# Linear attention and two MLPs on one core: the first block's attention in halves of 64 positions, and the low part of x by a matrix product

## The chip, the core and the metric

The kernel runs on one core of one Trainium2 chip. The metric is the device time of one execution in microseconds (us): 966.9 us before the change, the median of three runs (966.79 to 966.91 us).

Five engines work side by side, each through its own queue of instructions in order: PE (TensorE, matrix products into the accumulator memory PSUM), DVE (VectorE) and ACT (ScalarE) for element-wise work, POOL (GpSimd, here only constants), and SP (SyncE), which issues the transfers. Semaphores order them.

## What is computed

```python
def attn(q, k, v, alpha):                 # B=4, H=8, S=768, D=48
    state = zeros((B, H, D, D))
    for t in range(S):
        state = alpha[:, :, t, :, None] * state + einsum('bhd,bhe->bhde', k[:, :, t], v[:, :, t])
        y[:, :, t] = einsum('bhd,bhde->bhe', q[:, :, t], state)
x = y as (3072, 384)
x = ((x @ w_a) * (x @ w_b)) @ w_out       # 384 -> 1536 -> 384
h = x @ w_in                              # 384 -> 2048
out = (max(h, 0) + beta * min(h, 0)) @ w_out2
```

## The kernel before

**Blocks and chunks.** The 3072 tokens are worked in 6 blocks of 512. A block holds 4 chunks of 128 positions, one for each of the 4 sequences of the batch, so that the chunks of a block do not depend on each other and each takes its state from the chunk of the same sequence in the block ahead. The attention of a chunk comes first (`chunk`, L359), then the two products of the first MLP over the whole block (`pa`, `pb`), then its third (`acc`); after all blocks, the second MLP runs over weights that were written to memory in between.

**Two parts of a number.** The large products are made in a fast format (fp32r), so each operand is a high part, which is the rounded number, and a low part, which is what is left; one product of 128x512 is three matrix products (high times high, low times high, high times low: L699, L700, L702). The weights arrive as 64-bit numbers and are cut into these parts by `conv` (L231): an ACT operation, four DVE operations, an ACT rounding, and then the low part, which is made on DVE, or, for the first unit of each weight (the list `ON_PE`), by three products with the identity on PE (L308 to L310) and an ACT copy. Two of these first units are worked in halves of 384 columns (`halves`).

**A chunk.** DVE makes two scans of the decay (L402, L412) and multiplies k and q by them (L417). PE transposes k (`kps`, L453), ACT copies it out (`ks`). PE multiplies k with q (`A`), DVE masks the result (`As`), PE multiplies it with v (`y`), adds the state's part (`inter`), and computes the chunk's state sum (`dS`). ACT rounds y to the high part of x (`split_h`, L657), DVE subtracts it for the low part (`split_l`, L661).

**Three kinds of block.** Blocks 1 to 5 work a chunk in two halves of 64 positions: `pe_cross` (each half's own key rows against the other head group, and the two half states), then `z1`, the state in the chunk's middle (`mid`, DVE), then `pe_own` (L558 again, then L565 with Z, then L565 with z1). The array's four quarters are used at once: a product on 64 partitions in and 64 out takes one quarter, and in these loops two following indices change the quarter each time. Block 0 has no state to start from and takes each chunk whole: `A` over 128 columns (L471), `pe_d` (L528) and `pe_y` (L544, and L548 with `vg`, a copy of v that holds the fourth group's rows where the first three leave room). Block 0 thus needs no fourth group of 128 rows; block 1 moves the fourth group into these places by a product with `shift` (L611), and the later blocks by transfers (L677).

**What sets the order.** Nothing is scheduled by hand. Each operation is handed to a planner (`Graph`) with an engine, an estimated duration and a key; it walks its estimates and emits each engine's queue in that order. Where PE would be idle for over 500 ns by its estimates, it emits small products on a constant (`wp`, L185), up to the start of block 2, for about 0.7 of the gap that it expects. They are emitted as ordinary work: on the chip they run whether PE would have waited or not.

**Where the first block's buffers are.** In block 0 `kps`, and the two halves of `A`, use the three banks that later accumulate the MLP (`acc0` to `acc2`); `y` uses a pair of banks of its own, one pair for all chunks, held until the low part of x is made.

Of the kernel before, what the change touches and what calls it, by code (L numbers as in the profile page):

```python
# [11 lines left out]
F32 = mybir.dt.float32  # L12
# [9 lines left out]
P = 128  # L22
# [117 lines left out]
def body(tc, akq, v, vg, w_a, w_b, w_o1, w_in, w_o2, beta, out):  # L140
# [13 lines left out]
    with ExitStack() as ctx:  # L154
# [12 lines left out]
        mask = const.tile([P, P], F32, name="mask")  # L167
# [10 lines left out]
        def fill(t0, t1):  # L178
# [13 lines left out]
        nc.gpsimd.affine_select(  # L192
            out=mask, in_=mask, pattern=[[1, P]], compare_op=ALU.is_ge, fill=0.0,
            base=0, channel_multiplier=-1,
        )
# [28 lines left out]
        def conv(src, tag, name, key, wait, sink, early=15000, on_pe=False, halves=None):  # L224
# [14 lines left out]
            for n in range(2 if halves else 1):  # L239
# [29 lines left out]
                def rest(c2=c2, word=word):  # L269
                    o = c2()  # L270
                    nc.vector.scalar_tensor_tensor(out=o, in0=word(0, U32), scalar=2.0**-52,
                                                   in1=c2(), op0=ALU.mult, op1=ALU.mult)

                def high(n=n, c1=c1, hi=hi):
                    if n == 0:
                        b["r"] = wpool.tile([P, 2 * UC], F32R, name=f"w{name}", tag=tag)
# [24 lines left out]
                for h in range(2 // N):  # L301
# [3 lines left out]
                    def add(p=p, cut=cut, c1=c1, c2=c2, hi=hi):  # L305
# [4 lines left out]
                        nc.tensor.matmul(o, ident, cut(c2()), start=False, stop=True)  # L310
# [5 lines left out]
                    y = G.add("PE", 1600, add, key, [x], pool=mpool)  # L316
# [37 lines left out]
        def chunk(g):  # L354
            s = st[g]
            n, c = divmod(g, BC)
            start, moved, end = n == 0, n == 1, n == NB - 1
# [40 lines left out]
            lv = A("SP", 1250 if start else 720, load_v, vring.take(), 12000, 3000)  # L398
# [66 lines left out]
            def pe_a():  # L465
                if start:
                    s["A"] = [b(f"A{i}") for i, b in enumerate(abanks)]
                    for j in range(NJ):
                        for i in range(2):
                            ps = slice(64 * i, 64 * i + D)  # L470
                            nc.tensor.matmul(s["A"][i][:, j, :], kT()[ps, j, :], qT()[ps, j, :],  # L471
                                             start=True, stop=True)
                    return
# [10 lines left out]
            def ev_a(i):  # L484
                def f():
                    if i == 0:
                        s["At"] = tp.tile([P, 2 * NJ * CH], F32, name="As", tag="As", bufs=1)
                        w = CH if start else HC
                        s["As"] = s["At"][:, 0 : 2 * NJ * w].rearrange("p (i j t) -> p i j t", i=2, j=NJ)
                    if start:  # L490
                        m = mask.rearrange("p (o t) -> p o t", o=1).to_broadcast([P, NJ, CH])
                        nc.vector.tensor_tensor(out=s["As"][:, i], in0=s["A"][i], in1=m, op=ALU.mult)
                        return
                    m = mask[:, 0:HC].rearrange("p (a o t) -> p a o t", a=1, o=1).to_broadcast([P, 2, NJ, HC])
                    a = s["A"].rearrange("p i (j t) -> p i j t", t=HC)
                    nc.vector.tensor_tensor(out=s["As"], in0=a, in1=m, op=ALU.mult)
                return f

            w = sring.take()
            if start:  # L500
                (b0, w0, h0), (b1, w1, h1) = bank(1), bank(2)
                abanks = (b0, b1)
                pa = A("PE", 1200, pe_a, [k1, q1, *w0, *w1])
                a0 = A("DVE", 660, ev_a(0), [pa, *w])
# [517 lines left out]
```

## Time and profile before

| what | before |
|---|---|
| median of 3 runs | 966.9 us (966.79 to 966.91) |
| the profiled execution, its own time | 966.85 us |
| its span, first to last instruction | 965.2 us |
| PE busy | 952.7 us, 99% of the span |
| DVE busy | 600.4 us, 62% |
| ACT busy | 253.9 us, 26% |
| granted TensorE clock, mean | 0.999 |

The time outside the span is 1.65 us. A row of the timeline gives the start, the duration, the engine, the line of the code, the operation, and what it writes and reads; xN is the number of instructions merged into it. A PE duration includes the pipeline behind the last instruction, so the cost of a group of PE work is taken from its start to the next group's start. An fp32 product leaves two records, so 8 of them show as x16.

### The profile page before, as it was taken

To read this page: it belongs to the slowest core of one execution; us is meant where nothing else is said; L and a number is where in the kernel's file an instruction comes from. 1 tells how busy PE (TensorE), PEld (TensorE's weight loads), DVE (VectorE), ACT (ScalarE), POOL (GpSimd) and SP (SyncE) were. 2 spreads that over 40 slices of the span, in tenths; PEclk is the share of its full clock that TensorE was granted. 3 is DMA by queue.
4 is the path that set the end of the run, shared out by engine and by line. 5 is a ranking of instruction groups with operands and counts; after the bars stand their busy time and mean duration, and the time that the engine had idled before them with its cause. 6 is when DMAs were issued, how large, how long until landed. Compare 5 with 4: busy or idle time off the path is not lost.

```text
span 965.2 us, 15549 instructions
## 1 busy us (share of the span) xinstructions
PE 952.7 (99%) x6667; PEld 770.4 (80%) x6667; DVE 600.4 (62%) x887; ACT 253.9 (26%) x422; POOL 4.4 (0%) x18
## 2 busy tenths in 40 slices
PE   6999999999999999999999999999999999999998
PEld 5778888778877887887788888888888888888886
DVE  7999888578668868865332254555555545545554
ACT  2444443233333333332221211111111111111111
POOL 1000000000000000000000000000000000000000
PEclk9999999999999999999999999999999999999999
DMA  8971000145456545742065550010100200200000
GB/s 317 407 287 51 12 1 12 45 145 180 150 179 204 206 167 191 240 153 79 25 210 197 196 196 1 27 72 1 65 33 1 89 10 0 99 1 1 33 1 33
DMA packets 31076, 104.09 MB, mean 108 GB/s; under 512 B 3488, under 2 KB 4256, under 8 KB 31008
## 3 DMA queue, kind: packets, MB, share of 16 engines
q1 hardware_dynamic: 30864, 102.97, 30.2%
q8 instruction: 52, 0.85, 0.4%
q10 hardware_dynamic: 144, 0.13, 0.0%
q14 instruction: 16, 0.13, 0.0%
HBM read 74.78 MB, written 26.74 MB: 105 GB/s over the span
## 4 chain that ended last, share of the span: by engine, by line
PE 99%; DVE 0%; DMA 0%; ACT 0%; issue 0%; DVEq 0%; ACTq 0%
PE acc L699 12%; PE acc L702 12%; PE acc L700 12%; PE pi L699 7%; PE pi L702 7%; PE pi L700 7%; PE pb L699 5%; PE pa L699 5%; PE pa L700 5%; PE pb L700 5%; PE pb L702 5%; PE pa L702 5%; PE wp L185 2%; PE y L558 2%; PE kps L453 1%; PE A L481 1%
## 5 line engine op out<-in xcount | busy, mean ns | idle before, releaser
L722 ACT CAST gh<-ng 128x512 fp32r<-128x512 f32 x96 | 59.6, 621 | 328.6 <-DVE ng L935 275.0
L931 DVE TENSOR_SCALAR ng<-pi,betaT 128x512 f32<-128x512 f32 x96 | 72.1, 751 | 106.7 <-PE pi L702 105.8
L726 DVE TENSOR_TENSOR gl<-ng,gh 128x512 fp32r<-128x512 f32 x96 | 66.3, 691 | 79.9 <-ACT gh L722 79.9
L699 PE MATMUL pi<-x,v 128*128 128x512 f32 x288 | 113.3, 393 | 0.0
L700 PE MATMUL acc<-gh,v 128*128 128x512 f32 x288 | 113.1, 393 | 0.0
L702 PE MATMUL acc<-gl,v 128*128 128x512 f32 x288 | 112.9, 392 | 0.0
L700 PE MATMUL pi<-x,v 128*128 128x512 f32 x288 | 112.7, 391 | 0.0
L699 PE MATMUL acc<-gh,v 128*128 128x512 f32 x288 | 112.1, 389 | 0.0
L829 DVE TENSOR_TENSOR a_sb<-a_sb,pb 128x512 f32<-128x512 f32 x72 | 49.4, 686 | 96.5 <-PE pb L702 96.4
L699 PE MATMUL pa<-x,wa 128*128 128x512 f32 x216 | 86.7, 401 | 0.0
L699 PE MATMUL pb<-x,wb 128*128 128x512 f32 x216 | 86.6, 401 | 0.0
L699 PE MATMUL acc<-gh,wo 128*128 128x512 f32 x216 | 86.6, 401 | 0.0
L702 PE MATMUL acc<-gl,wo 128*128 128x512 f32 x216 | 84.9, 393 | 0.0
L700 PE MATMUL pa<-x,wa 128*128 128x512 f32 x216 | 84.7, 392 | 0.0
L700 PE MATMUL pb<-x,wb 128*128 128x512 f32 x216 | 84.6, 392 | 0.0
L700 PE MATMUL acc<-gh,wo 128*128 128x512 f32 x216 | 84.6, 392 | 0.0
L826 ACT COPY a_sb<-pa 128x512 f32<-128x512 f32 x72 | 42.2, 587 | 151.0 <-PE pa L702 151.0
L702 PE MATMUL pi<-x,v 128*128 128x512 f32 x288 | 81.5, 391 | 0.0
L722 ACT CAST gh<-a_sb 128x512 fp32r<-128x512 f32 x72 | 44.8, 622 | 102.6 <-DVE a_sb L829 102.6
L935 DVE SCALAR_TENSOR_TENSOR ng<-pi,ng 128x512 f32<-128x512 f32 x96 | 66.4, 691 | 3.1
L699 PEld LDWEIGHTS pi<-x,v 128*128 128x128 f32 x288 | 54.1, 188 | 13.7 <-DVE ng L935 2.1
L699 PEld LDWEIGHTS acc<-gh,v 128*128 128x128 f32 x288 | 54.0, 188 | 12.3
(120 smaller groups left out, 1426.5 us busy)
## 6 DMA issues: line engine op xcount, KB each, us to landing
kq<-in_akq SPq DMA_DIRECT2D x24, 512.0 KB, 3.8
w2d<-ws SPq DMA_DIRECT2D x16, 768.0 KB, 3.5
v<-w2d SPq DMA_DIRECT2D x16, 768.0 KB, 5.4
x2d<-x SPq DMA_DIRECT2D x18, 512.0 KB, 3.3
x<-x2d SPq DMA_DIRECT2D x6, 1536.0 KB, 6.9
ra<-in_akq SPq DMA_DIRECT2D x24, 258.5 KB, 3.5
v<-in_v SPq DMA_DIRECT2D x24, 256.0 KB, 4.4
rs<-in_w_in SPq DMA_DIRECT2D x8, 768.0 KB, 5.5
```

The lines of the kernel that those rows point to most:

```text
L185: nc.tensor.matmul(wp, warm[:, 0:P], warm, start=True, stop=True)
L453: nc.tensor.transpose(s["kps"][:, j, :], kT()[:, j, :], ident)
L558: nc.tensor.matmul(y_of(k, half(p), part_of(h)), s["v"][part_of(h), 2 * j + i, :], s["As"][part_of(h), i, j, :], start=first, stop=False, ...
L699: nc.tensor.matmul(o, lh, rh, start=first and n == 0, stop=False)
L700: nc.tensor.matmul(o, ll, rh, start=False, stop=False)
L702: nc.tensor.matmul(o, lh, rl, start=False, stop=last and n == len(pairs) - 1)
L722: nc.scalar.copy(gq[idx][0], src())
L726: nc.vector.tensor_tensor(out=gl, in0=src(), in1=gh.bitcast(F32), op=ALU.subtract)
L826: nc.scalar.copy(b["a"], ba["t"])
L829: nc.vector.tensor_tensor(out=b["a"], in0=b["a"], in1=bb["t"], op=ALU.mult)
L931: nc.vector.tensor_scalar(out=b["n"], in0=bh["t"], scalar1=0.0, scalar2=betaT[:, i : i + 1], op0=ALU.min, op1=ALU.mult)
L935: nc.vector.scalar_tensor_tensor(out=b["n"], in0=bh["t"], scalar=0.0, in1=b["n"], op0=ALU.max, op1=ALU.add)
```

## The change

Five things are done, all of them ahead of block 2, but for one order of products that all blocks share.

1. The first units of `w_a` and `w_b` (the ones in halves) round their smallest part at once into the place of the low part, and the third product of the three on PE then takes that rounded part in the fast format, where it took an fp32 operand.
2. Block 0 works its chunks in halves of 64 like the others. `A` is made as in blocks 1 to 5, one mask operation stands where two were, the mask constant is made in halves, and the ACT copy that halved it is gone. There is no state at the start, so `inter` runs for the second half alone. The half states are separate products (`state_of`), the first in `pe_cross`, the second in `pe_own`, summed in one PSUM region; ACT copies them out (`mid`, `kept`).
3. `y` of block 0 uses the banks `acc1` and `acc2`, held until the low part of x has been copied out; the shared pair of banks holds `A`.
4. `vg` is gone, its 4 transfers and its products with it; block 0 moves the fourth group by the product with `shift`, as block 1 does.
5. In blocks 0 and 1 the low part of x is made by PE, which adds minus the high part onto y in PSUM (`less`), and ACT, which copies the result out (`ev_l`).

In `pe_own` of all blocks the order is new: the second half's `inter` for the even heads (`i` = 0, upper half of the array), the eight `intra`, the second half's `inter` for the odd heads (lower half), and then the first half's `inter`.

```diff
-                def rest(c2=c2, word=word):
-                    o = c2()
+                def rest(n=n, c2=c2, lo=lo, word=word):
+                    if n == 0 and halves:
+                        b["r"] = wpool.tile([P, 2 * UC], F32R, name=f"w{name}", tag=tag)
+                    o = lo() if halves else c2()
...
-                        nc.tensor.matmul(o, ident, cut(c2()), start=False, stop=True)
+                        rest = (plus, cut(lo())) if halves else (ident, cut(c2()))
+                        nc.tensor.matmul(o, *rest, start=False, stop=True)
...
-            start, moved, end = n == 0, n == 1, n == NB - 1
+            start, moved, end = n == 0, n <= 1, n == NB - 1
...
-                if start:
-                    s["vg"] = wpool.tile([P, KT, 2, 64], F32, name="vg", tag=f"s{c % 2}")
-                    nc.sync.dma_start(s["vg"], vg[c])
...
+            def inter(j, i, h, last):
+                k, p = slot_of_head(j, i)
+                ps = slice(64 * i, 64 * i + D)
+                z = s["z1"] if h else Z[:, c]
+                nc.tensor.matmul(y_of(k, slice(64 * p, 64 * p + D), part_of(h)), z[ps, j, :],
+                                 qT()[ps, j, part_of(h)], start=False, stop=last,
+                                 skip_group_check=True)
+
+            def state_of(h):
+                for j in range(NJ):
+                    for i in range(2):
+                        nc.tensor.matmul(s["dS"][h][half(i), j, :], s["ks"][part_of(h), j, half(i)],
+                                         s["v"][part_of(h), 2 * j + i, 0:D], start=False,
+                                         stop=j == NJ - 1, skip_group_check=True)
...
+                for j in range(NJ):
+                    for h in range(2):
+                        intra(j, 1 - h, h, j < 2)
+                if start or end:
+                    state_of(0)
+                    return
...
+            def pe_own():
+                for j in range(NJ):
+                    inter(j, 0, 1, False)
+                for j in range(NJ):
+                    for i in range(2):
+                        intra(j, i, i, False)
+                for j in range(NJ):
+                    inter(j, 1, 1, j > 1)
+                if start:
+                    state_of(1)
+                    return
+                for j in range(NJ):
+                    for i in range(2):
+                        inter(j, i, 0, j > 1)
...
-                def pe_own():
-                    for j in range(NJ):
-                        for i in range(2):
-                            intra(j, i, i, False)
-                    for h, z in ((0, Z[:, c]), (1, s["z1"])):
-                        for j in range(NJ):
-                            for i in range(2):
-                                inter(j, i, h, z, h == 1 and j > 1)
...
+            def less():
+                for x, y in two(0):
+                    nc.tensor.matmul(y, minus, x, start=False, stop=True, skip_group_check=True)
+
+            def ev_l():
+                for x, y in two(1):
+                    nc.scalar.copy(x, y)
...
-            xl = A("DVE", 700, split_l, [s["xh"]])
-            yhold.append(xl)
+            if moved:
+                xl = A("PE", 450, less, [s["xh"]])
+                xl = A("ACT", 700, ev_l, [xl])
+            else:
+                xl = A("DVE", 700, split_l, [s["xh"]])
```

How the queues change is shown at three places. PE's queue around the second chunk of block 0, before (`A_240` and `A_241` are the two banks of `A`):

```order
L453 MATMUL kps<-plus,kq 128x128 x4
L544 MATMUL y<-As,v 64x128 x6
L548 MATMUL y<-As,vg 64x128 x6
L471 MATMUL A_240<-kq 128x128
L471 MATMUL A_241<-kq 128x128
...
L528 MATMUL dS<-v,ks 64x48 x8
```

and after the change, the first chunk's `pe_cross` to its `less` (`y_211` and `y_212` are the two banks of its y; the `kps` and `A` in it belong to the second chunk):

```order
L517 MATMUL y_212<-v,ks 64x48 x8
L455 MATMUL kps<-plus,kq 128x128 x4
L475 MATMUL A<-kq 64x64 x16
L510 MATMUL y_211<-kq,As 48x64 x4
...
L510 MATMUL y_212<-kq,As 48x64 x4
L517 MATMUL y_212<-v,ks 64x48 x8
...
L584 MATMUL y_211<-shift 128x128 x2
L584 MATMUL y_212<-shift 128x128
...
L636 MATMUL y_211<-x,minus 128x256
L636 MATMUL y_212<-x,minus 128x128
```

The 12 products over `v` and `vg` became 16 `intra`, 8 `inter` and 3 `shift`; the one state became two, of 8 products each; `less` is new.

PE's queue at a chunk of a later block, its `pe_own`, before:

```order
L558 MATMUL y<-As,v 64x64 x8
L565 MATMUL y<-kq,Z 48x64 x8
L565 MATMUL y<-kq,As 48x64 x8
L453 MATMUL kps<-plus,kq 128x128 x4
L699 MATMUL pa<-x,wa_1652 128x512
```

and after:

```order
L510 MATMUL y<-kq,As 48x64 x4
L502 MATMUL y<-As,v 64x64 x8
L510 MATMUL y<-kq,As 48x64 x4
L510 MATMUL y<-kq,Z 48x64 x8
L455 MATMUL kps<-plus,kq 128x128 x4
```

The same 24 products stand in another order: the 8 over `z1` (it lies in the tile `As`) are parted in two fours, one ahead of the `intra` and one behind.

ACT's queue from the first chunk's `ks` on, before:

```order
L457 COPY ks<-kps 128x512
L630 COPY Z<-dS 128x192
L457 COPY ks<-kps 128x512
L657 CAST x<-y 128x2x128
L657 CAST x<-y 128x128
```

and after (`As<-y_212` is z1, `shift<-y_212` the fourth group that is to be moved):

```order
L459 COPY ks<-kps 128x512
L547 COPY As<-y_212 128x192
L580 COPY shift<-y_212 128x128
L603 COPY Z<-y_212 128x192
L459 COPY ks<-kps 128x512
L628 CAST x<-y_211 128x2x128
L628 CAST x<-y_212 128x128
L256 ACTIVATE c_316<-ra_192 128x3x128
L640 CAST x<-y_211 128x2x128
L640 CAST x<-y_212 128x128
```

ACT has four operations more for each chunk of block 0, and a weight conversion's first operation (L256) now stands between the rounding of x and the copy of its low part.

In the whole program PE's queue has 128 `wp` where it had 125; from the first `pa` of block 1 on, the large products stand in the same order as before, and the chunks of blocks 2 to 5 differ by `pe_own` alone.

## Rows read from the trace of the kernel before

**Rows 1.** The page's first part: busy time and share of the span.

```profile
PE 952.7 (99%) x6667; PEld 770.4 (80%) x6667; DVE 600.4 (62%) x887; ACT 253.9 (26%) x422; POOL 4.4 (0%) x18
```

**Rows 2.** Waits, whole span: who waited, for whom, us in total, times, longest.

```profile
PE kps L453 <- DVE kq L417: 8.0, 1, 8.0
```

**Rows 3.** Timeline of PE, the first 21 us: start, duration, instructions.

```profile
7.96 1.09 PE L453 MATMUL kps<-plus,kq 128*128 128x128 f32 x4 [7.96 <-DVE kq L417]
...
12.01 2.83 PE L185 MATMUL wp<-ones 128*128 128x256 bf16 x13
14.68 0.60 PE L453 MATMUL kps<-plus,kq 128*128 128x128 f32 x4
15.21 0.88 PE L544 MATMUL y<-As,v 128*64 128x128 f32 x12
...
16.67 1.16 PE L471 MATMUL A<-kq 48*128 48x128 f32 x16
17.76 0.67 PE L528 MATMUL dS<-v,ks 128*64 128x48 f32 x16
18.36 2.36 PE L185 MATMUL wp<-ones 128*128 128x256 bf16 x20
20.56 0.60 PE L453 MATMUL kps<-plus,kq 128*128 128x128 f32 x4
```

**Rows 4.** The tile wp: all its products, duration in ns, first and last start.

```profile
L185 PE MATMUL wp<-ones x125: 271/272/421, 12.0 to 89.2; 128*128 128x256 bf16 x125
```

**Rows 5.** Timeline of PE: one conversion's three products in halves.

```profile
29.18 0.91 PE L308 MATMUL cl<-c,plus 128*128 128x384 f32 x2
...
30.11 0.81 PE L310 MATMUL cl<-c,plus 128*128 128x384 f32 x2
30.75 0.49 PE L185 MATMUL wp<-ones 128*128 128x256 bf16 x3
```

**Rows 6.** Timeline of PE: A in halves, and the first large product.

```profile
34.73 0.69 PE L481 MATMUL A<-kq 48*64 48x64 f32 x32
35.35 0.51 PE L699 MATMUL pa<-x,wa 128*128 128x512 f32 x1
```

**Rows 7.** Timeline of PE: a chunk of block 1, half states and pe_own.

```profile
41.45 0.63 PE L581 MATMUL y<-v,ks 64*64 64x48 f32 x32
...
43.67 0.46 PE L558 MATMUL y<-As,v 64*64 64x64 f32 x16
43.96 0.41 PE L565 MATMUL y<-kq,Z 48*48 48x64 f32 x16
44.18 0.40 PE L565 MATMUL y<-kq,As 48*48 48x64 f32 x16
```

**Rows 8.** Timeline of PE: a product with shift, and what follows it.

```profile
58.78 0.83 PE L611 MATMUL y<-shift 128*128 128x128 f32 x6
59.45 0.81 PE L308 MATMUL cl<-c,plus 128*128 128x384 f32 x2
```

**Rows 9.** Timeline of PE: block 5, one half state alone, then a large product.

```profile
438.67 0.63 PE L581 MATMUL y<-v,ks 64*64 64x48 f32 x16
439.23 0.50 PE L699 MATMUL pb<-x,wb 128*128 128x512 f32 x1
```

**Rows 10.** Stretches of L558's eight products: length; PE and PEld busy (records under way).

```profile
84.59:84.62 0.03, 0.03 (x4) 0.03 (x4) 1.00 0.00 0
84.63:84.70 0.07, 0.07 (x4) 0.07 (x8) 1.00 0.00 0
```

**Rows 11.** Timeline of PE: the first large product of block 1.

```profile
89.21 0.48 PE L699 MATMUL pa<-x,wa 128*128 128x512 f32 x1
```

**Rows 12.** Timeline of ACT: the rounding of x after the first y.

```profile
16.78 0.54 ACT L657 CAST x<-y 128x256 fp32r<-128x256 f32 x2 [0.83 <-PE y L548]
```

**Rows 13.** Groups to 90 us: instructions, busy us, mean ns, idle before.

```profile
L661 DVE TENSOR_TENSOR x<-y,x 128x256 fp32r<-128x256 f32 (+1 forms) x16 | 4.9, 349 | 0.2 <-ACT x L657 0.2
...
L607 ACT COPY shift<-y 128x128 f32<-128x128 f32 x4 | 1.1, 274 | 1.7 <-PE y L565 1.7
```

More of the change, by code (lines that the diff above doesn't have):

```diff
@@ L274, in high @@
                 def high(n=n, c1=c1, hi=hi):
-                    if n == 0:
+                    if n == 0 and not halves:
                         b["r"] = wpool.tile([P, 2 * UC], F32R, name=f"w{name}", tag=tag)
@@ L397, in chunk @@
             lq = A("SP", 1400, load_kq, lwait, 13800, 3000, [la])
-            lv = A("SP", 1250 if start else 720, load_v, vring.take(), 12000, 3000)
+            lv = A("SP", 720, load_v, vring.take(), 12000, 3000)
             def scan_r():
@@ new lines, in mid @@
+            def mid():
+                s["z1"] = s["At"][:, 2 * NJ * HC :].rearrange("p (j d) -> p j d", d=D)
+                if start:
+                    nc.scalar.copy(s["z1"], s["dS"][0])
+                else:
+                    nc.vector.tensor_tensor(out=s["z1"], in0=s["dS"][0], in1=Z[:, c, :, :], op=ALU.add)
+            def pe_own():
[6 more added lines that the diff above has]
+                    inter(j, 1, 1, j > 1)
+                if start:
+                    state_of(1)
+                    return
+                for j in range(NJ):
+                    for i in range(2):
+                        inter(j, i, 0, j > 1)
@@ L604, in chunk @@
+            if start:
+                (b0, w0, h0), (b1, w1, h1) = bank(1), bank(2)
+                ybanks, w = (b0, b1), [*w0, *w1]
+            else:
+                w, h0, h1 = pring.take(), pring.last(), []
+            pc = A("PE", 850, pe_cross, [a0, ks, lv, *w])
+            kring.use(pc)
+            z1 = A("ACT" if start else "DVE", 360, mid, [pc, zs])
+            py = A("PE", 850, pe_own, [z1, zs, q1])
+            kring.use(py)
+            own = py
             if moved:
@@ L629, in kept @@
                     if start:
-                        nc.scalar.copy(z, s["dS"])
+                        nc.scalar.copy(z, s["dS"][1])
                     else:
                         nc.vector.tensor_tensor(out=z, in0=s["dS"][1], in1=s["z1"], op=ALU.add)
-                x = A("ACT" if start else "DVE", 360, kept, [ds] if start else [z1, py])
-                (dhold if start else yhold).append(x)
+                x = A("ACT" if start else "DVE", 360, kept, [z1, own])
+                for hold in (h0, h1):
+                    hold.append(x)
                 if not start:
@@ L638, in chunk @@
                 state[c] = [x]
-            nt = KT if start or moved else NJ
             sring.use(py)
@@ L681, in chunk @@
             xdone[n] = moves
-        masked, halved = [], []
         for g in range(NG):
-            if g == BC:
-                def halve():
-                    nc.scalar.copy(mask[HC:, 0:HC], mask[HC:, HC:])
-                halved.append(G.add("ACT", 250, halve, block_at[1] - 60000, masked))
             chunk(g)
```

158 lines of the change are left out of this document (45 added, 113 removed).

## The prediction, made before the changed kernel had run

> **What bounds the kernel now.** I read the page's busy shares first: PE is busy for 952.7 us, 99% of the span [rows 1]. Then the waits: PE waited once, for 8.0 us at the very start, for DVE's first k and q [rows 2]. That leaves about 4.5 us, the last copy and store after PE's last product. Then PE's timeline, row by row, to see whether "busy" hides waits. It does not: the same group takes the same time from its start to the next start wherever it stands, and no row but the first carries an idle time [rows 3]. PE starts at 7.96 us and is never late for anything. What hides the waits of the start-up are the `wp` products: 125 of them, from 12.0 to 89.2 us [rows 4], which the planner put where its estimates saw PE idle. By the time they have run, what PE would have waited for is there.
>
> So the time is 8.0 us, plus every product that PE is given, `wp` included, plus the tail. In that regime only three things count: how much PE work is added or taken away, how many `wp`, and whether a wait appears that is longer than the `wp` ahead of it. Less work on DVE or ACT, a shorter transfer, a free buffer are worth nothing by themselves. The change takes 16 subtractions of together 4.9 us [rows 13] and four of eight mask operations from DVE; PE never waited for DVE after 7.96 us, so I count that as nothing. The cover is the planner's: were the `wp` fewer, it would show, but they go from 125 to 128. The four `vg` transfers count as nothing for the same reason: what waits for weights is DVE, and DVE is ahead of PE.
>
> The profiled execution took 966.85 us, 1.65 us of it outside the span, and agrees with the median of 966.9; I sum against 966.85.
>
> **Block 0, each chunk.** Removed: y with `vg`, 15.21 to 16.67, 1.46 us; A, 16.67 to 17.76, 1.09 us; the state, to 18.36, 0.60 us [rows 3]. Sum 3.15 us. Added: A in halves 0.62 us [rows 6]. In `pe_cross` eight `intra`, 0.29 us [rows 7], and a half state alone: block 5 shows one, 0.56 us from its start to the next [rows 9]. It is as long as the full two half states of block 1 (0.63 us as a row, 32 records against 16 [rows 7, 9]), because it uses the upper half of the array only. `pe_own`: the lower half has the most to do, two rounds of `intra`, two of `inter` and a half state, and a group of two rounds takes 0.22 us [rows 7], so 0.22 + 0.22 + 0.56 = 1.0 us. The product with `shift` 0.67 us [rows 8]. `less` is new: 384 columns in the fast format. Twenty `wp` of 256 columns take 2.20 us, 0.11 each [rows 3], so 0.17 us, which is the lower bound; I take 0.25 for the change of format, with 0.4 as the upper bound. Sum 3.39 us. Four chunks: +1.0 us.
>
> **Block 1.** Four `less`, +1.0 us (0.7 to 1.6).
>
> **The conversions.** The three products take 1.57 us, the last of them 0.64 us, an fp32 operand that leaves two records [rows 5]. In the fast format 384 columns are 0.17 us by the `wp`. Four of them: -1.9 us (if the format's change costs something, -1.2).
>
> **The fills.** Three more: +0.3 us.
>
> **The slow start.** The first 13 `wp` take 2.67 us, 205 ns each, against 110 ns later [rows 3]: up to about 14.6 us the products run at the lower of TensorE's two levels (1.2 against 2.4 GHz), though the profile's clock line does not mark it. The first k and q come no earlier, so PE starts at 7.96 again and is as dense; I take the slow stretch as unchanged. Were it over where the 15 `wp` of the new order begin, 15 times 95 ns, 1.4 us, would be gained; as much could be lost.
>
> **New waits.** In block 0 a chunk now passes from PE to ACT and back four times: z1, the moved group, the high part, the low part. ACT begins 0.11 us after y is done and rounds it in 0.54 us [rows 3, 12]; a small copy takes 0.27 us [rows 13]. With 0.11 for each hand-over the chain from `pe_cross` to the low part is 0.85 + 0.27 + 1.0 + 0.27 + 0.67 + 0.54 + 0.25 + 0.54 and eight hand-overs of 0.11, 5.3 us, and the next chunk's `pe_cross` waits for its end, since y's two banks are held that long. Behind a waiting `pe_cross` stands all of PE's queue. Between two of them PE has 3.39 us of the chunk, `kps`, 0.53 us [rows 3], one or two conversions of 1.1 us and some 16 `wp` of 0.11 us, 6 us or more: the chain ends first, by little. What I expect to show are places where ACT, in order, has something else ahead, a conversion's operation or a copy of the accumulators. I take 0.5 us for all of them; the bounds are 0, since before the change there was none, and 2.4 us, 0.3 us at each of eight chunks.
>
> Sum: +1.0 + 1.0 - 1.9 + 0.3 + 0.5 = +0.9 us, 967.7 us, all of it ahead of the first large product of block 1, which starts at 89.21 us [rows 11] and from which on the large products are the same in the same order.
>
> **The order in pe_own, 20 chunks.** Here I had to choose. Before, every following product took another quarter of the array. Now the first four all go to the upper half, and the next four over z1 to the lower. Each quarter still gets six of the 24 products, so if the quarters work for themselves, nothing changes. If PE takes the products strictly in order, the first four block the queue for two rounds in half of the array, 0.22 us [rows 7] with the other half empty, and what the lower half does later is not made up. The trace shows how far PE runs ahead: four records begin within 30 ns and none in the 70 ns after [rows 10]. Every product leaves two records (16 for eight [rows 7]) and the code changes the quarter with each product, so a product's second part begins after the first parts of the next three. Strict order is thus not what happens; running three products ahead is shown, and five would be needed here.
>
> The Trainium skill has a rule on each side. "TensorE: Matmul & The Clock Gate", in the part on packing small matmuls, says that matmuls start and end in program order and only weight loads are pulled ahead; by it the first rival holds. "TensorEngine Tiling (Array Packing)", Key Properties, says that tiles operate independently, loads and matmuls alike; by it the forecast stands. Rows 10 agree with the second, as far as they reach.
>
> **The rivals.** (1) PE does not look five products ahead: 20 chunks of blocks 1 to 5 at +0.22 us and four `pe_own` of block 0 at +0.22 us, +5.3 us, of which the 0.5 us of waits is taken up: 972.5 us, slower by 0.6%. It decides from the first late product on the lower half; for it speaks that nothing in the trace shows five ahead, against it rows 10. (2) The chain over ACT is longer than I count: if ACT's queue puts a weight operation of half to one us into it at each chunk of block 0, the 5.3 us become 6 to 6.5 and PE waits about 0.8 us four times: 970.9 us. Against it: ACT is busy for only 26% [rows 1], though that is a mean over the span. (3) The change pays: the slow stretch ends early (-1.4 us), no wait appears (-0.5), `less` costs its lower bound (-0.6) and the shorter third product brings all (-0.3): 964.9 us, just faster by 0.2%. For it speaks only that the early `wp` stand closer to the start. (4) Less work on DVE shows after all: it would need PE to wait for DVE in the start-up, and no row has that.
>
> **Chances.** The forecast 0.60, 966.2 to 969.2 us by its own bounds; (1) 0.25; (2) 0.08; (3) and what I do not see in that direction 0.07. About 0.2% (1.9 us) is what a measurement of this kernel can tell from no change. The forecast is 0.9 us above, so one in seven of its cases is slower by more: same 0.52, slower 0.08 + 0.25 + 0.08 = 0.41, faster 0.07. The range leaves out some of (3) and the top of (1): 965.6 to 972.6 us.
>
> **What would show it.** PE's first product at 7.96; 15 `wp` at about 205 ns behind the first `A`; the first `pa` of block 1 at about 90.5 us with the 0.53 us of a `kps` that now stands ahead of it; the third product of a halved conversion at about 0.17 us; few and short idle times on PE, at `pe_cross`, `shift` and `less` in block 0. In blocks 2 to 5 the 24 products of a `pe_own` at about 0.8 us, three groups of 0.22 to 0.29 us [rows 7] (forecast), or at about 1.0 us (rival 1): this alone separates the two. Wrong would be idle PE of more than 2 us in all, or a first `pa` of block 1 before 88 us.

## The result: 979.2 us for 966.9, and the profile after

The changed kernel took 979.17 us (median of 4 runs, 978.08 to 980.13) against 966.9 (966.79 to 966.91): a ratio of 1.0127, interval 1.0109 to 1.0144. The forecast was 967.7 with a range up to 972.6. It is slower by more than any case I had priced. Ratios here and below leave out two single executions that took far longer than the others of their kernel (one of e1 with 3121.59 us, one of e6 with 1177.74 us).

The profiled execution after took 978.08 us. The page's busy shares and its clock line, to be held against [rows 1]:

```profile
PE 958.7 (98%) x6930; PEld 777.0 (80%) x6930; DVE 595.1 (61%) x883; ACT 259.9 (27%) x461; POOL 5.6 (1%) x19
...
PEclk9999999999999899999999999999999999999999
```

PE's busy time grew by 6.0 us, the span by 11.2, so its work alone does not explain the loss; and the clock line has an 8 in its 14th slice, where before there was none. I then laid the large products of the two traces side by side, the n-th of one against the n-th of the other (they are the same, in the same order but for two neighbouring groups of nine, the 68th and 69th, at the end of block 1, that change places). Up to the first of block 1 the changed kernel loses 2.1 us, 0.5 of which is a `kps` that now stands ahead of that point; through blocks 1 and 2 it drifts by fractions of a microsecond at each chunk; at the first large product of block 3 it falls 9 us further behind at once. This is PE's timeline there in the changed kernel (start, duration, instruction, idle before it and what ended that):

```profile
315.77 0.36 PE L510 MATMUL y<-kq,As 48*48 48x64 f32 x5
...
316.42 0.41 PE L510 MATMUL y<-kq,Z 48*48 48x64 f32 x12
316.76 0.66 PE L455 MATMUL kps<-plus,kq 128*128 128x128 f32 x4
318.73 0.69 PE L475 MATMUL A<-kq 48*64 48x64 f32 x32 [1.31 <-DVE x L632]
321.23 0.46 PE L502 MATMUL y<-As,v 64*64 64x64 f32 x16 [1.80 <-DVE As L483]
321.51 0.63 PE L540 MATMUL y<-v,ks 64*64 64x48 f32 x32
323.23 1.12 PE L455 MATMUL kps<-plus,kq 128*128 128x128 f32 x4 [1.09 <-DVE kq L419]
325.45 0.77 PE L677 MATMUL pa<-x,wa 128*128 128x512 f32 x1 [1.11 <-DMA x<-x]
326.02 0.63 PE L678 MATMUL pa<-x,wa 128*128 128x512 f32 x1
326.44 0.63 PE L677 MATMUL pa<-x,wa 128*128 128x512 f32 x1
```

At 315.77 the last chunk of block 3 does its own products; the last large product of block 2 is already over, and nothing large stands between here and the first `pa` of block 3. That `pa` needs x of the whole block: rounded, its low part subtracted, and the fourth group moved by six DMAs. The small groups in between belong to block 4; the planner put them into the hole, and three of them wait for DVE in their turn, before `pa` itself waits for a move. The four waits sum to 5.3 us of the 9; the rest is the small groups themselves, which stood elsewhere before, so part of it comes back later. The same place before the change, and the six moves as SP issued them, before and after:

```profile
305.07 0.46 PE L558 MATMUL y<-As,v 64*64 64x64 f32 x16
305.35 0.41 PE L565 MATMUL y<-kq,Z 48*48 48x64 f32 x16
305.58 0.40 PE L565 MATMUL y<-kq,As 48*48 48x64 f32 x16
305.91 0.50 PE L699 MATMUL pb<-x,wb 128*128 128x512 f32 x1
...
314.49 0.40 PE L702 MATMUL acc<-gl,wo 128*128 128x512 f32 x1
314.82 0.69 PE L481 MATMUL A<-kq 48*64 48x64 f32 x32
315.44 0.50 PE L699 MATMUL pa<-x,wa 128*128 128x512 f32 x1
```

```profile
308.55 3.88 SPq L677 DMA_DIRECT2D x<-x  x6
```

```profile
318.65 5.34 SPq L661 DMA_DIRECT2D x<-x  x6
```

Before, 36 large matmuls (four groups of nine) stood between the same own products and the `pa`, and hid the whole chain: the moves went out at 308.55, the last landed at 314.22, and `pa` followed at 315.44 without a wait. There was 1.2 us to spare, no more.

Behind the hole the matmuls run slowly. Three stretches of the changed kernel (PE busy, PEld, DVE, ACT, POOL, then the granted clock):

```profile
317.00:323.00 6.00, 2.03 (x84) 1.56 (x82) 5.43 (x8) 2.51 (x5) 0.00 (x0) 0.97 0.87 275
323.00:326.00 3.00, 1.66 (x5) 1.22 (x6) 3.00 (x6) 0.00 (x0) 0.00 (x0) 0.50 0.71 143
326.00:330.00 4.00, 4.00 (x12) 3.12 (x11) 1.88 (x4) 0.37 (x1) 0.00 (x0) 0.57 0.96 325
```

After 6 us in which PE was busy for 2.0, the granted clock is 0.50, the lower level (1.2 against 2.4 GHz), up to shortly before 330 us. The large products there follow each other every 0.43 us and not every 0.23: nine of them take 1.8 us longer. The slow `kps` at 323.23 (1.12 us for 0.66) adds half a microsecond of slow work, but it ends before the move lands for which `pa` waits, so a fast one would only have waited longer. (The 2.4 us that the expectations of e1 and e12 give are the two together.)

At the start, the forecast's own markers: PE began at 7.90, for 7.96 before [rows 3], and the 15 `wp` that now come first ran from 9.98 to 12.68, 180 ns each in the mean, where 13 had run at 205: every 213 ns up to 11.9 us, every 110 ns from there on. So in this execution the slow stretch ended nearer 12 than 14.6 us: a gain of about a microsecond that I had only as a bound.

### The profile page after: what moved, and what is told of

Same layout as the page of the kernel before. It is cut to its first block, busy times and chain, and to the rows that moved or that the text cites. A ratio compares the mean times of both kernels' runs of the same rounds, so it can differ in the third digit from the quotient of the medians.

```text
span 976.4 us, 16119 instructions
## 1 busy us (share of the span) xinstructions
PE 958.7 (98%) x6930; PEld 777.0 (80%) x6930; DVE 595.1 (61%) x883; ACT 259.9 (27%) x461; POOL 5.6 (1%) x19
## 4 chain that ended last, share of the span: by engine, by line
PE 97%; DVE 1%; DMA 1%; issue 0%; ACT 0%; SPq 0%; ACTq 0%; DVEq 0%
PE acc L677 12%; PE acc L678 12%; PE acc L680 12%; PE pi L677 7%; PE pi L678 7%; PE pi L680 7%; PE pa L677 5%; PE pb L677 5%; PE pa L678 5%; PE pa L680 5%; PE pb L678 5%; PE pb L680 5%; PE y L510 2%; PE y L502 2%; PE A L475 1%; PE wp L185 1%
```

## The experiments

Thirteen kernels. Each states its edit against the kernel that it names. The line that most of them turn on is the planner's key for a chunk (L363 after, L358 before): the plan takes, on each engine, the ready operation with the smallest key, and starts are worked out from the durations written in the code. The plan's own times are not chip times; here they tell only what stands before what.

### Where the 12 us are: place, order, and both

Theory A: three causes, the place of block 3's last chunk, the order in `pe_own`, and the start-up. The rivals stand with each run.

**e1_key3**, the changed kernel with block 3's chunks due 500 ns earlier:

```diff
-            key = block_at[n] - (BC - c) * 9500 - 6000 if n else c * 1000 - 100000
+            key = block_at[n] - (BC - c) * 9500 - 6000 - 500 * (n == 3) if n else c * 1000 - 100000
```

> The changed kernel with one number in the planner's keys: the four chunks of block 3 are due 500 ns earlier. By the plan the last chunk's own products of block 3 then stand four large products ahead of the end of block 2's, as before the change, and not behind the last of them. Theory A (the place of that chunk): the idle PE time at the change to block 3 (1.31 + 1.80 + 1.09 + 1.11 = 5.3 us) and the half clock behind it (about 2.4 us) go, 979.2 becomes about 971.5 (970.5 to 972.5), and no product runs at the lower clock behind 300 us. Theory B (the loss is spread over the twenty chunks, 0.15 us or more each, with start-up): the time stays at 978 to 979.5. Theory C (the clock falls by itself, because PE's load changed): the stall goes but products at the lower clock stay, about 974.

Measured: 971.13 us, ratio to before 1.0042 (1.0029 to 1.0056). PE's waits in this run, complete:

```profile
PE kps L455 <- DVE kq L419: 7.8, 1, 7.8
PE A L475 <- issue: 0.4, 1, 0.4
PE y L510 <- DVE As L549: 0.2, 1, 0.2
```

The four waits at block 3 are gone, the own products of its last chunk start at 307.5 and 36 large matmuls stand behind them again, and no large product behind 300 us runs at the lower level. Half a microsecond in a key is worth 8.0 us. Theories B and C fall.

**e2_old_own**, the changed kernel with the old order of own products from block 1 on:

```diff
+                if not start:
+                    for j in range(NJ):
+                        for i in range(2):
+                            intra(j, i, i, False)
+                    for h in range(2):
+                        for j in range(NJ):
+                            for i in range(2):
+                                inter(j, i, h, h == 1 and j > 1)
+                    return
```

> The changed kernel with the order of own products before the change in blocks 1 to 5 (all within-half products first, then the upper halves, then the lower); the first block and every chunk's place stay as changed. Theory A (the order costs 0.15 us a chunk, since the engine looks only part of the way ahead): twenty chunks give 3.0 us back, less what lies in the stall: 976.0 to 977.0. Rival (the own groups look longer in the records, but their neighbours get shorter by as much): 979. The forecast's rival of 0.22 us each: 974.8. The stall at block 3 stays in all of them.

Measured: 976.09 us (1.0095). 3.1 us come back; a `pe_own` takes 0.84 us as before, and the stall is still there (waits of 1.3, 1.8, 0.5 and 1.0 us).

**e3_key3_old_own**, both edits:

> Both edits: block 3 due 500 ns earlier and the old order of own products. Theory A: 966.9 + 1.6 of start-up = 968.5, 967.8 to 969.5, so that the three causes (start-up 1.6, order 3.0, place with stall and clock 7.7) add up. If the causes overlap (the old order alone shortens the stall), the sum of the two single gains is over what this run gives back, by 1 us or more.

Measured: 968.68 us (1.0023, 1.0014 to 1.0032), as theory A says. From 979.17 to 971.13 by the place, to 968.68 by the order; what is left to 966.94 is 1.7 us. The sum of the single gains (8.0 + 3.1) is 0.6 us over what both give, less than the 1 us that would have meant an overlap.

**e4_less_block1**, the kernel before with one part of the change, block 1's low part:

```diff
-            xl = A("DVE", 700, split_l, [s["xh"]])
+            if moved:
+                xl = A("PE", 450, less, [s["xh"]])
+                xl = A("ACT", 700, ev_l, [xl])
+            else:
+                xl = A("DVE", 700, split_l, [s["xh"]])
```

> The kernel before with one part of the change: the low part of x of block 1 by a product with minus one and a ScalarE copy. Nothing of block 0, the conversions or the own order is changed. By the plan this alone puts block 2's last chunks one large product earlier and block 3's last chunk behind the last large product of block 2. Theory A: 966.9 + 0.4 to 1.1 for the products + 7.7 for the stall and the clock: 975 to 976. Rival (the place needs the whole change, or the stall needs the new own order): 967.3 to 968.

Measured: 975.14 us (1.0086, 1.0072 to 1.0099). Eight small matmuls and eight copies in block 1, which end at 88 us, make a stall of 4.6 us at 317 us. The way there is in the plan: block 2's last chunk comes one group of nine earlier, so SP issues the six moves of block 2 ahead of a load for block 3's second chunk, which was ahead of them before; that chunk's transposes miss their early place and run at 273.86 us where they ran at 227.74; and the own products of block 3's four chunks, which stood behind 90, 96, 100 and 104 of the 108 groups of large products that come before block 3, stand behind 90, 98, 103 and 108. In the changed kernel they stand at the same four places. (The profiled execution has another 1.6 us in it that is not from here; see the last section.)

**e12_late3**, the kernel before with block 3's chunks due 3000 ns later, none of the change in it:

```diff
+            key = block_at[n] - (BC - c) * 9500 - 6000 - (-3000) * (n == 3) if n else c * 1000 - 100000
```

> The kernel before with block 3 due 3000 ns later and nothing else. By the plan its last chunk's own products then stand 106 and not 104 large products of the plan ahead (108 are all that come before block 3's first; one is nine matmuls, 2.06 us). Theory A: before, 9.15 us lay between those own products' start (305.07) and the landing of the moves (314.22), and the first product of block 3 followed 1.2 us later, so there was no stall and little slack. With two products in the place of four, 0.84 + 2 x 2.06 + 0.36 + 0.62 = 5.9 us cover the 9.15: idle of 3.2 us, 969.5 to 971, and if the clock falls behind it, as behind the changed kernel's 5.3 us, 2.4 us more (972 to 973). Rival (the stall came from the changed kernel's parts, not from the place): 966.7.

Measured: 970.38 us against 966.41 (1.0036, 1.0022 to 1.0049): +4.0 us out of an untouched kernel. PE's timeline:

```profile
314.49 0.60 PE L453 MATMUL kps<-plus,kq 128*128 128x128 f32 x4
315.02 0.70 PE L481 MATMUL A<-kq 48*64 48x64 f32 x32
316.09 0.47 PE L699 MATMUL pa<-x,wa 128*128 128x512 f32 x1 [0.38 <-DMA x<-x]
316.40 0.40 PE L700 MATMUL pa<-x,wa 128*128 128x512 f32 x1
317.35 0.47 PE L699 MATMUL pa<-x,wa 128*128 128x512 f32 x1 [0.55 <-DMA x<-x]
317.65 0.40 PE L700 MATMUL pa<-x,wa 128*128 128x512 f32 x1
318.72 0.47 PE L699 MATMUL pa<-x,wa 128*128 128x512 f32 x1 [0.67 <-DMA x<-x]
```

18 large matmuls stand in the place of 36, and `pa` waits for moves three times. Recorded idle is 1.6 us and not my 3.2, since each pair of products waits only for its own move. Two pieces more are idle without a mark: `A` to `pa` takes 1.07 us, with 0.62 elsewhere, and each second product of a pair is followed only after 0.95 to 1.07 us, which the marks cover in part. Behind it eight products run every 0.43 us. So the place alone makes a stall, and it grows as the cover shrinks: 36 large matmuls of cover, no loss; 18, four microseconds; none, eight (this last in the changed kernel, by e1).

### What an order of small products costs

**e5_orders**, the kernel before with five orders of the 24 products of `pe_own`, one to a block (block 1 as in the changed kernel); the loop for the others:

```diff
+                        w = {2: 2, 3: 4, 4: 12, 5: 6}[n]
+                        if n == 5:
+                            rows = [r[0::2] + r[1::2] for r in rows]
+                        for k in range(0, 12, w):
+                            for i in range(2):
+                                for f, a in rows[i][k : k + w]:
+                                    f(*a)
```

> The kernel before, where the 24 own products of a chunk are issued in another order in each block: block 1 in the changed kernel's order, block 2 two products of the upper row half and two of the lower by turns, block 3 four and four, block 4 twelve and twelve, block 5 six and six by quarter of the array. The sums are the same. Before, each took 0.84 us with four quarters by turns. If the engine can hold every quarter's queue apart (what the forecast took), all five stay at 0.84 us. If it starts nothing out of order, one quarter's product takes 0.84 / 6 = 0.14 us and the groups take about 1.1 (block 1), 0.84 (block 2), 0.98 (block 3), 1.7 (block 4) and 3.0 us or more (block 5). If it looks a few products ahead (theory, from the 0.99 us of the changed kernel): 0.99, 0.84, 0.84 to 0.9, 1.3 to 1.6, 2.5 to 3.2 us.

Measured, from the group's start to the next group's start, the same to 0.01 us in all four chunks of a block: 0.99, 0.84, 0.88, 1.35 and 2.36 us. The sum over before is 4 x (0.15 + 0 + 0.04 + 0.51 + 1.52) = 8.9 us; the run, a single execution, took 975.11, 8.5 us over the median of before. The theory of a limited look-ahead holds; both extremes fall. How far it goes is seen in block 4, where all twelve products of the upper half are issued ahead of the lower's (L558 within the half, L565 over Z and over z1, which lies in the tile As):

```profile
354.02 0.45 PE L558 MATMUL y<-As,v 64*64 64x64 f32 x8
354.30 0.39 PE L565 MATMUL y<-kq,Z 48*48 48x64 f32 x8
354.53 0.22 PE L565 MATMUL y<-kq,As 48*48 48x64 f32 x2
354.54 0.27 PE L558 MATMUL y<-As,v 64*64 64x64 f32 x2
354.58 0.28 PE L565 MATMUL y<-kq,As 48*48 48x64 f32 x4
354.65 0.22 PE L558 MATMUL y<-As,v 64*64 64x64 f32 x2
```

At 354.54 the lower half's first products (`As,v` again) begin, ahead of the upper half's last (`kq,As` at 354.58), which were issued before them. So products do start out of order, but only when the half in front has about 0.3 us of its 0.84 left (the last three of its twelve products not yet begun): the other half stands empty for the first 0.5 us. The Trainium skill's "TensorE: Matmul & The Clock Gate" (on packing small matmuls) has matmuls starting and ending in program order, "TensorEngine Tiling (Array Packing)", Key Properties, has tiles working independently; these rows agree with neither as it stands.

### The parts of the start-up

**e6_conversion**, the kernel before with the conversion's third product in the fast format:

```diff
-                        nc.tensor.matmul(o, ident, cut(c2()), start=False, stop=True)
+                        rest = (plus, cut(lo())) if halves else (ident, cut(c2()))
+                        nc.tensor.matmul(o, *rest, start=False, stop=True)
...
-                    y = G.add("PE", 1600, add, key, [x], pool=mpool)
+                    y = G.add("PE", 1100 if halves else 1600, add, key, [x], pool=mpool)
```

> The kernel before with the conversion edit alone (the third product of each conversion group in the fast format, its planned time 1100 for 1600). No chunk changes its place among the large products behind block 1. Forecast term: four products of about 0.65 us become 0.17, 1.9 us off a PE-bound stretch: 965.0. Rival (the conversions lie in time in which PE would have been filled with warm-up products): 966.9, no change.

Measured: 966.02 us, 0.6 below before, ratio 1.0001 (0.9977 to 1.0024): by that, no change that can be told. The interval is this wide through one execution of 977.38 us at a granted clock of 0.949. The nine that are left have a mean of 965.4 us, 1.2 below the mean of before, though they spread from 963.98 to 966.48; in the profiled one, the shortest, the first large product of block 1 came at 86.5 for 89.2. So a gain of about a microsecond is likely, below the forecast's 1.9.

**e7_all_but_block0**, the kernel before with the conversion, block 1's low part, and block 3 due 500 ns earlier (edits as above):

> The kernel before with the conversion edit, with the low part of block 1 by a product and a ScalarE copy, and with block 3 due 500 ns earlier; block 0 (with its gathered v) and the order of own products as before. Theory A: the start-up's loss is all block 0's, so this run is faster than before by the conversions and by what the vector engine is spared in block 1 (start-up 0.8 us shorter in the run with that alone): 964.2, 963.5 to 965.5. Rival (block 0 costs nothing and the two other edits don't pay): 967 to 968.7.

Measured: 965.91 us (0.9995, 0.9987 to 1.0004): not the 964.2 of the sum, not the rival's loss.

**e8_block0_halves**, block 0 in halves without `vg` and nothing else of the change (the changed kernel with the other parts put back):

> The changed kernel with the conversions, both blocks' low parts (on VectorE again) and the own order of blocks 1 to 5 as before: what stays of the change is block 0 in halves of 64 with its state summed in PSUM and no gathered v, moved by three shift products as in block 1. By the plan no later chunk changes its place. Theory A (block 0 in halves loses what the run with key and old order lost beside the gains of the other parts): 966.9 + 1.8 + 1.9 + 0.8, less four products of 0.3 us for the low part: about 970. Rival by the forecast's own term (3.15 us a chunk become 3.09): 966.7.

Measured: 965.66 us (0.9990, 0.9981 to 0.9999), the opposite of what I wrote: by itself it gains 1.0 us. So the parts tried by themselves are each worth about a microsecond of gain or nothing, and all of them together, with key and old order (e3), lose 1.7. The parts don't add up.

**e9_low0, e10_low_none, e11_low1** make a square: the changed kernel with the old own order, the low part of block 0 and of block 1 each by product and copy, or by DVE (the condition of `less` is `start`, `False` or `n == 1` for `moved`). e11 and e3 have the key of e1 too; e9 and e10 need none, and in none of the four does PE wait at block 3.

> The changed kernel with the old order of own products, and block 1's low part on VectorE again; block 0 in halves, its low part by a product and a ScalarE copy, and the conversions stay as changed. No key is changed: by the plan the later chunks stand where they stood before the change. Beside the two runs below it fills a square of four (low part of block 0, of block 1, each by product or by VectorE) whose fourth corner, both by product, took 968.7. Theory S (the end of the start-up is the chain of block 1's last chunk, and only block 1's low part lies in it): 964.5 to 966, as fast as the corner with neither. Rival (block 0's chain delays the first large products, and that is not caught up): 967 to 968.5, by 0.5 us a chunk.

> The same with both blocks' low parts on VectorE: block 0 in halves and the conversions are all that stays of the change. Alone they gave -1.0 and -0.7 us. Theory S: they add up as long as PE is behind with large products, 965.2 (964.5 to 966). If both shorten the same wait, 965.7, no better than the halves alone. This is the candidate for a version faster than the kernel before.

> The changed kernel with the old own order and block 3 due 500 ns earlier, block 0's low part on VectorE and block 1's by product and ScalarE copy. Theory S: the loss is all here, the two more hops of the last chunk (PE's product, ScalarE's copy) lie bare in front of the first large product of block 1: 967.5 to 969, near the corner with both (968.7). Rival (block 0's low part is what costs): 965 to 966.

| low part by product in | time, us | ratio to before | last large product ended | next began | `wp` |
|---|---|---|---|---|---|
| no block (e10) | 966.01 | 0.9988 (0.9979 to 0.9997) | 85.2 | 89.5 | 120 |
| block 0 (e9) | **963.21** | 0.9962 (0.9948 to 0.9975) | 80.5 | 85.8 | 88 |
| block 1 (e11) | 965.74 | 0.9989 (0.9980 to 0.9998) | 82.5 | 88.7 | 121 |
| both (e3) | 968.68 | 1.0023 (1.0014 to 1.0032) | 79.1 | 91.7 | 128 |

The last three columns are from the traces: the end of the last large product that can run ahead of block 1, the start of block 1's first, and the number of fills. Against e10, moving one low part away from DVE brings the last large product *earlier* by 2.6 or 4.7 us, both by 6.1. (1.6 us of each is an idle piece of PE in the profiled execution of e10, the slowest of its eleven, that the others lack; no cause is recorded for it.) In these stretches PE had been waiting for weights that DVE converts, and `wp` covered it. In e10, 25 `wp` and a chunk's products lie ahead of the first `pb` over a new unit of `w_b`, whose low part DVE finishes 0.2 us before that `pb` starts:

```profile
66.92 1.92 PE L185 MATMUL wp<-ones 128*128 128x256 bf16 x16
...
69.61 1.16 PE L185 MATMUL wp<-ones 128*128 128x256 bf16 x9
70.53 0.48 PE L681 MATMUL pb<-x,wb 128*128 128x512 f32 x1
```

```profile
69.39 0.95 DVE L287 TENSOR_TENSOR wb<-c,c 128x768 fp32r<-128x768 f32 x1
```

In e9 the same low part is done at 63.85, its `pb` starts at 65.85, and no `wp` stands between 41 and 81 us:

```profile
62.90 0.95 DVE L287 TENSOR_TENSOR wb<-c,c 128x768 fp32r<-128x768 f32 x1
```

```profile
65.85 0.50 PE L681 MATMUL pb<-x,wb 128*128 128x512 f32 x1
```

PE has four `less` more in e9 than in e10 but 32 `wp` fewer: the planner's estimates saw the shorter wait too. And all five executions of e9 (962.5 to 963.9 us) are below all eleven of e10 (964.0 to 967.0).

With both moved, the stretch behind the last large product, in which only chunks and `wp` are left, grows from 4.3 to 12.6 us. My theory S (only block 1's low part costs) fell: beside block 0's by DVE it costs nothing. The stretch of e3, and the first half of PE's timeline in it (large products left out):

```profile
79.14:91.67 12.53, 12.18 (x214) 10.15 (x213) 12.53 (x21) 6.14 (x16) 0.00 (x0) 1.00 0.26 91
```

```profile
78.92 0.83 PE L588 MATMUL y<-shift 128*128 128x128 f32 x6
79.59 1.58 PE L185 MATMUL wp<-ones 128*128 128x256 bf16 x13
80.93 0.42 PE L640 MATMUL y<-x,minus 128*128 128x256 f32 x2
81.19 1.49 PE L185 MATMUL wp<-ones 128*128 128x256 bf16 x12
82.84 0.70 PE L475 MATMUL A<-kq 48*64 48x64 f32 x32 [0.16 <-ACT x L644]
83.47 1.60 PE L185 MATMUL wp<-ones 128*128 128x256 bf16 x13
```

and ACT in the same run:

```profile
79.79 0.55 ACT L632 CAST x<-y 128x256 fp32r<-128x256 f32 x2
81.43 0.93 ACT L256 ACTIVATE c<-ro 128x768 f32<-128x768 f32 x1 [1.09 <-DVE wa L287]
82.26 0.52 ACT L644 CAST x<-y 128x256 fp32r<-128x256 f32 x2
```

The third chunk's `shift` and `less` come after the last large product. Its low part on ACT (82.26) stands behind a weight operation that waits 1.09 us for DVE; the last chunk's `A` needs the banks that this frees (the mark at 82.84), and the whole last chunk follows bare, until 91.67. In e9 the last chunk's `A` ran at 77.56, under large products. In the plan the third chunk's own products stand behind 11 of the 12 large groups in e3, and behind 8 or 9 in the other three corners: the same kind of cause as at block 3. The next run tests it.

**e13_keys13**, e3 with block 1 due earlier too:

```diff
+            key = block_at[n] - (BC - c) * 9500 - 6000 - (500 if n == 3 else 5000 if n == 1 else 0) if n else c * 1000 - 100000
```

> The kernel of the third run (all of the change, old own order, block 3 due 500 ns earlier; 968.7) with block 1 due 5000 ns earlier too. By the plan the own products of block 1's third chunk then stand behind 9 and not 11 of the 12 groups of nine large products that there are ahead of block 1. Both low parts still go by product and ScalarE copy. Theory P (what the start-up loses is again the place: the last chunk's chain had nothing large left to lie beside): the stretch from the last large product of block 0 to the first of block 1 shrinks from 12.6 us to about 6, and the time to 965.5 to 966.5, as in the run with block 1's low part alone (965.7). Rival (the hops over PE and ScalarE in both blocks cost that time themselves, wherever the chunk stands): 968 to 969.

Measured: 966.54 us (0.9996, 0.9987 to 1.0005), at the upper end of theory P and clear of the rival's 968 to 969. The bare stretch went from 12.6 to 8.0 us, not to 6, and 2.1 us came back, of 2.2 to 3.2 expected. So the place is a good part of that loss; what the rest is was not tried. With two keys and the old own order the whole change is as fast as the kernel before. The fastest version is e9: everything but block 1's low part and the own order, 3.5 us below before.

## Why the prediction was wrong, point by point

**The sentence that failed** is the one under the sum: that all of the change's effect lies ahead of block 1's first large product, "from which on the large products are the same in the same order". But for two neighbouring groups they are. The chunks of blocks 2 to 5 stand between them, though, and I did not look where: that they differ "by `pe_own` alone", as the section on the change has it, is true of what is in them and not of their places. 8.0 of the 12.2 us are that (e1; e4 and e12 have the stall without the rest of the change). In the plan of the changed kernel the last own products of block 3 stand directly ahead of the block's first `pa`; the chain from there over the rounding, the low part and six moves had taken 9.15 us in the trace of before, and with 36 large matmuls behind it 1.2 us were to spare. Both could be read beforehand. The rivals had longer chains in block 0, none at a block's change.

**The order in pe_own.** Right was that PE does not go strictly in order, and that 24 products at 0.8 or 1.0 us would tell the cases apart. The choice was wrong: three products ahead was shown [rows 10], five were needed, and I took the step from three to five as likely. The price of rival 1 was 0.22 us; measured 0.15, in each of 20 chunks, 2.5 to 3.1 us in all (e2; e1 against e3).

**The regime.** The forecast let DVE's relief count as nothing, since PE "is never late", with one condition: were the `wp` fewer, it would show. In the start-up that ground was wrong. Rows of `wp` are waiting time in the look of work where PE waits for DVE's conversions behind them (e10 above), and 125 of them [rows 4] were no sign that it was never late. Moving block 0's low part from DVE to PE and ACT gave 2.8 us (e10 to e9). The forecast's own sum comes near that, once it is told that 32 fills of 0.11 us go and four `less` of 0.3 come, 2.3 us less; what it had wrong is that the number of fills stands by itself, when it follows DVE's work. My rival 4, for which "no row" spoke, was the mechanism of the gain. In the whole change, with 128 fills, that gain is lost again in the last chunk's bare chain.

**The terms of the start-up** were mostly well sized and belong to a sum that does not decide. By the rows after, each from its start to the next start, as forecast: `A` mostly 0.62, the half state 0.56, `shift` 0.67 to 0.77; `less` 0.18 to 0.35 (0.25 taken), the conversion's third product 0.18 to 0.27 (0.17 taken), the `wp` three more. Under-sized: the lower half's own products with their state, 1.19 to 1.22 us and not 1.0, in block 0's chunks. The slow stretch at the start ended about a microsecond's worth earlier, which I had as a bound. That the start-up's net loss came to 1.7 us against my 0.9 is chance: it is the bare chain of the last chunk, about 8 us longer, less 6 us by which the large products came earlier.

**The hidden stall and the clock.** I had priced no loss by the clock behind a stall. At block 3 it added 1.8 us behind 5.3 us of idle.

## What to carry to other kernels

Where a plan sets the order, compare the plan's *places* of every group with a long chain behind it, not the order within one kind of instruction; a change at 40 us can move a group at 300 us, and half a microsecond in a key can be worth eight. For every hand-over between stages write down the chain's length and the cover behind its start; a cover that exceeds the chain by 1.2 of 9 us is a stall waiting for the next edit. Filling products can be idle time: an engine that is 99% busy with them in it may be waiting, and work taken off the engine that it waits for can pay.

## What the runs showed of the hardware

**A clock that falls behind a broken stretch.** 5.3 us of idle in pieces of 1.1 to 1.8 us were followed by the lower level up to just before 330 us. Even 1.6 us of marked idle in three pieces (e12) had it: 0.73 granted in 320 to 325.

```profile
320.00:325.00 5.00, 5.00 (x18) 3.92 (x17) 3.55 (x5) 1.78 (x4) 0.00 (x0) 0.73 1.03 327
```

**Two rhythms at one clock.** Large matmuls mostly follow each other every 226, 229 and 232 ns by turns, mean 228.9. In the profiled executions of e4 and e7 they came every 233.3 ns from block 1's first large product up to block 2's first chunk, at a granted clock of 1.00, and then as always. In e4, whose first large product of block 1 began at 88.44 for 89.21 before, the same product reached 172.98 for 172.17:

```profile
88.44 0.48 PE L711 MATMUL pa<-x,wa 128*128 128x512 f32 x1
...
172.98 0.40 PE L711 MATMUL pa<-x,wa 128*128 128x512 f32 x1
```

That is 1.6 us over some 360 products, about as much as the parts of this change are worth. It was seen in two of the fifteen traces, one execution of each kernel; what sets the rhythm stays open, and nothing was tried on it.

**A small transfer behind large ones.** The six moves of 64 KB landed 2.3 to 2.4 us after their issue before; in the changed kernel, issued just behind a load and two stores of 512 KB each, the first took 6.5 us (318.65 to 325.11). The stores, issued at 317.26 and 317.88, landed at 322.07 and 323.53. That the moves were late because of them was not tried by itself.
